# Handing phase products to operand tiles inside SBUF, and loading the first W blocks earlier, in an FFT convolution followed by token mixing

## The chip, the cores and the metric

The kernel runs on one core of one Trainium2 chip. The metric is the time of one execution on the device in microseconds (us). The profiled execution is one of the timed ones; its span is about 1.7 us shorter than its time.

In the lines of the profile PE is TensorE, DVE VectorE, ACT ScalarE, POOL GpSimd, and SPq the queue of SyncE, which issues DMAs; L833 is line 833 of the kernel, x4 a count, and m, b, zz, y_ap are tiles by their names in the program (b an operand tile, zz the products of a step). HBM is the memory outside the core, SBUF the core's own, PSUM the place where TensorE's sums arise. The *issue* of a DMA is the time that an engine takes to start it; it *lands* when its data has arrived. A wait is given to what ended it last.

## The reference

x is 8 × 5696 × 128 (batch, tokens S, channels), h is 5696 × 128, the two token-mixing matrices are 5696 × 5696 each.

```python
# stage 1: causal convolution along the tokens, by FFT of length 2*S
y  = irfft(rfft(x, 2*S) * rfft(h, 2*S)[None])[:, :S, :]
# stage 2
theta  = y @ w_theta
zr, zi = y * cos(theta), y * sin(theta)
u = y + einsum('ts,bsd->btd', w_tok_r, zr) + einsum('ts,bsd->btd', w_tok_i, zi)
out = u + relu(u @ w_ch)
```

## The kernel before

It has three parts that follow one another, with overlaps.

1. **FFT stages** (to about 462 us). The last inverse stage writes y, channel-major, to HBM (`yt_hbm`) and to SBUF.
2. **Phase steps** (in part beside the last inverse stage, then alone to about 550 us). One step handles 128 tokens of one half of the batch (4 of 8). The 22 token tiles of the first pass make 44 steps. A step transposes y, forms theta in PSUM, lets ScalarE take the sines and VectorE the products, writes y to HBM (`y2_hbm`), and hands zr and zi on, in two blocks of 64 tokens.
3. **Token mixing**, in two passes over the source tokens. The right-hand operand of a pass is 11 tiles b0 to b10, each of four blocks of 64 tokens, and of sums of its parts (the kernel multiplies by a scheme of seven products in place of eight; the very first visit, `tt == 0`, uses plain products while the sums are still being made). W comes in blocks, converted to bf16 by DMAs that GpSimd issues, into six slots, and is transposed by VectorE.

The hand-over from part 2 to part 3 goes through HBM: a step writes its products, and the tile is fetched whole after its last write.

```python
# in a phase step
def copy():
    nc.vector.tensor_copy(y_ap, tpz)
    nc.sync.dma_start(y2_hbm[ti]...[:, 512 * hh:512 * hh + 512], y_ap...)
...
nc.scalar.activation(mag, r, AF.Abs)
nc.scalar.activation(red, r, AF.Sin, bias=zero_b[:m], scale=-TWO_PI)
nc.scalar.activation(mag, mag, AF.Sin, bias=half_pi[:m], scale=-TWO_PI)
...
zi_eng.tensor_mul(zi, red, yflat)
nc.vector.tensor_mul(zr, mag, yflat)
for e in range((m + 63) // 64):                       # two blocks of 64 tokens
    ...
    nc.sync.dma_start(z_hbm[:, p_, j, i, :, cols].rearrange("z t n -> t z n"), zz[rows])
```

```python
# operand tiles; the eight early ones (NE) are fetched between the steps of the second half
def load_b(p, j, pool):
    t_ = pool.tile([P, 7 * 1024], BF16, tag=f"b{j}", name=f"b{j}")
    for z in range(2):
        eng = nc.scalar if p or j >= NE else nc.sync
        eng.dma_start(t_[:, z * 2048:(z + 1) * 2048],
                      z_hbm[z, p, j].rearrange("i (s r) n -> (i s) (r n)", r=2))   # rows of 4 KB
...
for n, ti in enumerate(tile_order):
    phase_step(ti, 1)
    if n % 4 == 3:
        while len(bts_of[0]) < min(n // 2, NE):
            load_b(0, len(bts_of[0]), bpe)
```

```python
# the first W blocks wait for an operand tile, so as not to crowd the phase steps
after = bts_of[0][2][M2][:, 0, :2] if k == 0 else None
...
if after is not None:
    nc.gpsimd.tensor_copy(wb[:, 0, :2], after)
for i in range(4):
    nc.gpsimd.dma_start(wb[32 * i:32 * i + 32, :ng, :nj * 64], bass.AP(tensor=a.tensor, ...))
```

## Time and profile before

| | before |
|---|---|
| median of the first 3 runs | 2174.2 us (2172.3 to 2176.88) |
| span of the profiled run | 2175.5 us |
| end of the last inverse stage (issue of the last write of yt) | 462.6 us |
| first product of the mixing | 549.4 us |
| TensorE busy, 600 to 800 us | 198.95 of 200 us |

The span is read as a chain of stretches. In the two passes TensorE is nearly full, so this change can pay only in the two places that it touches and where TensorE stands: between the last inverse stage and the first product, and around 1340 us, where the second pass fetches its 11 tiles. The prediction below shows the first place in full. For the second, these are TensorE's waits of the kernel before from 600 us to the end (engine, line, what it waited for, then us in total, times, longest):

```profile
PE m L833 <- DMA b<-z_hbm: 4.0, 2, 2.0
...
PE m L831 <- DMA b<-z_hbm: 0.4, 1, 0.4
```

And this is its DMA view from 1325 to 1370 us: the queue that carries the reload (packets, MB, share of the time of 16 engines), then the loads (KB each, median us from issue to landing).

```profile
q10 hardware_dynamic: 2568, 9.33, 53.3%
...
b<-z_hbm ACTq DMA_DIRECT2D x12, 512.0 KB, 11.1
```

TensorE loses 4.4 us to this reload, though it moves some 11.5 MB (22 loads of 512 KB).

### The profile page before, as it was taken

The page shows a single profiled execution, that of the slowest core. Times are in us where ns is not written, and L with a number is a line of the kernel's source. Part 1 is how long each engine was busy: PE and PEld are TensorE (multiplying, and loading weights), DVE is VectorE, ACT ScalarE, POOL GpSimd, SP SyncE. Part 2 cuts the span into 40 slices and gives each one's busy share as a digit, 9 for nine tenths or more (in the row PEclk, how much of TensorE's full clock was granted, in tenths as well). Part 3 has the DMA queues.
Part 4 walks back from the last instruction along what each step waited for, and adds up shares of the span by engine and source line. Part 5 has one row for each costly group of instructions (what it writes and reads, how often), then busy time and mean ns, then how long its engine had stood idle before and what let it go on. Part 6 is the DMA issues. An engine that isn't in the chain of part 4 may idle for free.

```text
span 2175.5 us, 41105 instructions
## 1 busy us (share of the span) xinstructions
PE 1998.2 (92%) x15545; PEld 1125.1 (52%) x15723; DVE 1619.4 (74%) x2920; ACT 670.6 (31%) x984; POOL 857.1 (39%) x1572
## 2 busy tenths in 40 slices
PE   4788898763899999999999999899999999999998
PEld 4787888652344444444444444344444444444444
DVE  7767767767778888888877667667777777776867
ACT  5877877574132333333210000001111111111111
POOL 5301010002344645445466544354545453535350
PEclk8788889987899999999999999999999999999999
DMA  7356463579988989899999869687878787879794
GB/s 146 89 125 163 128 162 118 172 185 275 236 156 175 182 169 168 167 179 176 176 169 162 138 115 291 106 133 137 148 132 152 132 151 130 152 131 153 126 158 91
DMA packets 409382, 340.38 MB, mean 156 GB/s; under 512 B 83303, under 2 KB 363751, under 8 KB 408071
## 3 DMA queue, kind: packets, MB, share of 16 engines
q0 software_dynamic: 221312, 143.00, 48.7%
q1 hardware_dynamic: 183552, 179.93, 28.5%
q10 hardware_dynamic: 4320, 14.81, 1.8%
q8 instruction: 123, 2.02, 0.4%
q14 instruction: 75, 0.61, 0.1%
HBM read 381.83 MB, written 97.93 MB: 221 GB/s over the span
## 4 chain that ended last, share of the span: by engine, by line
PE 65%; DMA 5%; DVE 4%; issue 2%; ACT 2%; POOL 1%; SPq 1%; DVEq 0%; ACTq 0%; POOLq 0%
PE m L910 59%; DMA b<-z_hbm 3%; PE m L878 2%; DMA z_hbm<-zz 2%; DVE c L917 1%; PE v L680 1%; PE utp L673 1%; PE m L914 1%; DVE wt L591 1%; PE m L833 1%; POOL wb L582 1%; PE m L831 1%; ACT mag L404 0%; ACT red L405 0%; PE theta_ps L382 0%
## 5 line engine op out<-in xcount | busy, mean ns | idle before, releaser
L582 POOL DMA_DIRECT2D wb<-in_moe_w_tok_i_dram x720 | 387.9, 547 | 679.3 <-DVE wt L591 602.6
L591 DVE STREAM_TRANSPOSE wt<-wb 128x384 f32<-128x384 f32 (+2 forms) x720 | 360.2, 524 | 117.1 <-PE m L910 71.2
L582 POOL DMA_DIRECT2D wb<-in_moe_w_tok_r_dram x720 | 386.6, 548 | 146.2 <-DVE wt L591 107.0
L910 PE MATMUL m<-b,wt 128*128 128x512 bf16 x1803 | 425.7, 381 | 7.1 <-DVE wt L591 2.4
L910 PEld LDWEIGHTS <-wt 128*128 128x128 bf16 x1848 | 181.3, 98 | 225.0 <-issue 5.7
L917 DVE TENSOR_TENSOR c<-c,m 128x512 f32<-128x512 f32 x420 | 271.0, 671 | 0.4 <-PE m L910 0.4
L675 ACT ACTIVATE uts<-utp 128x512 bf16<-128x512 bf16 (+1 forms) x90 | 53.2, 592 | 607.3 <-PE utp L673 607.3
L320 PE MATMUL ps<-r_u,u_t 128*128 128x128 f16 x1024 | 133.0, 228 | 14.9 <-DVE u_t L304 11.7
L321 PE MATMUL ps<-r_v,v_t 128*128 128x128 f16 x1024 | 131.7, 227 | 0.0
L670 ACT ACTIVATE ub<-c 128x512 bf16<-128x512 f32 (+1 forms) x90 | 56.3, 628 | 224.9 <-DVE c L846 139.7
L127 POOL DMA_DIRECT2D x<-in_x_dram x64 | 34.2, 541 | 201.3 <-PE ps L190 189.3
L320 PEld LDWEIGHTS <-u_t 128*128 128x128 f16 x1024 | 106.0, 103 | 13.6 <-DVE u_t L304 13.5
L321 PEld LDWEIGHTS <-v_t 128*128 128x128 f16 x1024 | 104.9, 103 | 5.2 <-issue 3.7
L304 DVE TENSOR_TENSOR u_t<-xs,hs 128x1024 f16<-128x1024 f16 x96 | 69.6, 725 | 41.9 <-ACT xs L302 31.5
L302 ACT ACTIVATE xs<-ps 128x1024 f16<-128x1024 f32 x96 | 95.3, 1017 | 17.6 <-DVE v_t L304 8.7
L878 PE MATMUL m<-b,wt 128*128 128x512 bf16 x344 | 79.3, 387 | 15.3 <-ACT red L405 14.5
L190 PE MATMUL ps<-f_t,x 89*128 89x180 f16 x512 | 84.5, 310 | 8.0 <-ACT xs L302 5.9
L208 PEld LDWEIGHTS <-w_t 64*128 64x128 f16 x3240 | 65.5, 106 | 38.1 <-issue 24.7
L580 POOL COPY wb<-b 128x2 bf16<-128x2 bf16 x4 | 0.5, 179 | 213.2 <-DMA z_hbm<-zz 213.2
L190 PEld LDWEIGHTS <-x 89*128 89x128 f16 x512 | 73.8, 237 | 10.1 <-issue 9.4
L384 ACT ACTIVATE red<-theta_ps,magic 128x512 f32<-128x512 f32 (+1 forms) x46 | 31.6, 687 | 140.8 <-PE theta_ps L382 107.4
L623 ACT ACTIVATE yb<-tpz 128x512 bf16<-128x512 bf16 (+1 forms) x46 | 27.4, 597 | 153.6 <-PE tpz L621 137.4
(2713 smaller groups left out, 3824.5 us busy)
## 6 DMA issues: line engine op xcount, KB each, us to landing
wb<-in_moe_w_tok_r_dram POOLq DMA_DIRECT2D x352, 96.0 KB, 4.5
wb<-in_moe_w_tok_i_dram POOLq DMA_DIRECT2D x352, 96.0 KB, 5.0
wb<-in_moe_w_tok_r_dram POOLq DMA_DIRECT2D x352, 80.0 KB, 4.2
wb<-in_moe_w_tok_i_dram POOLq DMA_DIRECT2D x352, 80.0 KB, 3.7
hs<-hf_hbm SPq DMA_DIRECT2D x192, 128.0 KB, 3.2
cp_hbm<-c SPq DMA_DIRECT2D x88, 256.0 KB, 2.3
c<-cp_hbm SPq DMA_DIRECT2D x88, 256.0 KB, 4.0
out_dram<-c SPq DMA_DIRECT2D x88, 256.0 KB, 4.2
```

Source lines behind the costliest of these rows:

```text
L190: nc.tensor.matmul(ps[:, i // 2, (i % 2) * 2 * K1:(i % 2 + 1) * 2 * K1], lhs(q + i), f1_t[:NB], start=True, stop=True)
L208: nc.tensor.matmul(ps[:, e, j * HD:(j + 1) * HD], w_t2[rows, c0 + j, N2 * (1 - ri):N2 * (3 - ri)], a_st["a"][rows, ri * K1 + c0 + j, :], s ...
L302: nc.scalar.activation(xs[:, :, :, :ck], ps, AF.Copy)
L304: nc.vector.tensor_tensor(uv[r][:, :, :, c0:c0 + ck], xs[:, :, :, :ck], hv[:, r:r + 1, :, :ck].to_broadcast([P, 2, HD, ck]), op=mult)
L320: nc.tensor.matmul(o, u_t[:, at:at + P], r_u, start=True, stop=False)
L321: nc.tensor.matmul(o, v_t[:, at:at + P], r_v, start=False, stop=True)
L582: nc.gpsimd.dma_start(wb[32 * i:32 * i + 32, :ng, :nj * 64], bass.AP(tensor=a.tensor, offset=a.offset + row0 * S + p * H + i * QR + j0 * 6 ...
L591: nc.vector.transpose(wt.rearrange("p j t r -> p (j t r)").bitcast(F32).rearrange("p (j g t) -> p g j t", j=TJ, g=4)[:, :ng, :nj], wb[:, : ...
L670: nc.scalar.activation(ub[:m].rearrange("p b d -> p (b d)"), c[:m], AF.Copy)
L878: nc.tensor.matmul(ms[n // 2 * 2 + h], a[n][:, j, :, r], bts[jj][n % 2 * 2 + h][:, r, :], start=(n % 2 == 0 and jj == 0 and r == 0), stop= ...
L910: nc.tensor.matmul(ms[q], a[q][:, j, :, r], bts[jj][q][:, r, :], start=(jj == 0 and r == 0), stop=(jj == NJ - 1 and r == 1 and q not in left))
L917: nc.vector.tensor_tensor(c, z, ms[q], op=op)
```

## The change

The intent is to take the HBM round trip out of the hand-over. For the second half of the batch, a step copies its products inside SBUF straight into the eight early tiles; the first half, which is written long before, is fetched in halves beforehand. So that such a half is contiguous, HBM holds the two halves of the batch apart, which makes the rows of every tile load 2 KB in place of 4 KB. The first six W blocks and tile b0 move into the room of the forward FFT's dead table, so that W can be loaded behind the last inverse stage.

```diff
-    z_hbm_h = nc.dram_tensor("z_hbm", (2, 2, 11, 4, 64, BD), BF16, kind="Internal")
+    z_hbm_h = nc.dram_tensor("z_hbm", (2, 2, 11, 2, 4, 64, BD // 2), BF16, kind="Internal")
...
-    w_t2 = fc.tile([P, K1, 3 * N2], F16)
+    w_t2 = keep.tile([P, K1, 3 * N2], F16, tag="keep", name="w_t2")
...
-            if tags is None:
-                nc.sync.dma_start(z_hbm[:, p_, j, i, :, cols].rearrange("z t n -> t z n"),
-                                  zz[rows])
+            if tags is None and j in home:
+                for r in range(2):
+                    nc.sync.dma_start(
+                        home[j][32 * i:32 * i + 32, :4096].rearrange("p (z q r n) -> p z q r n", z=2, q=2, r=2)[:, :, q_, r],
+                        zz[e * 64 + r:e * 64 + 64:2])
+            elif tags is None:
+                nc.sync.dma_start(z_hbm[:, p_, j, q_, i].rearrange("z t n -> t z n"), zz[rows])
...
+    def pump():
+        while ring["n"] < len(queue) and (ring["n"] < 6 or queue[ring["n"] - 6][0] in ring["read"]):
+            queue[ring["n"]][1]()
+    def open_ring():
+        ring["all"] = keep.tile([P, K1 * 3 * N2], BF16, tag="keep", name="ring")
+        pump()
...
+    def load_b_half(j):
+        t_ = home_of[j] = tile_b(0, j, bpe)
+        for z in range(2):
+            nc.sync.dma_start(t_[:, z * 2048:z * 2048 + 1024],
+                              z_hbm[z, 0, j, 0].rearrange("i (s r) n -> (i s) (r n)", r=2))
...
+    for j in range(NE - 1):
+        load_b_half(j)
     for step in steps0:
         step()
+    load_b_half(NE - 1)
     sides["phases"]["sby"] = pool("s2y4", 4, pha, reuse_waits="tile")
-    for n, ti in enumerate(tile_order):
+    for ti in tile_order:
         phase_step(ti, 1)
-        if n % 4 == 3:
-            while len(bts_of[0]) < min(n // 2, NE):
-                load_b(0, len(bts_of[0]), bpe)
... (the rest renames buffers, moves small buffers of the background work into the same room,
     and moves the queue of W loads into pump)
```

More of the change, by code (lines that the diff above doesn't have):

```diff
@@ L106 @@
     fx = pool("fft_x", 1, xin)
+    NE, WB, BT = 8, 6 * 4 * CJ * 64, 7 * 1024
+    keep = pool("keep", 1, ctx, side="right")
     fc = pool("fft_c", 1, conv, side="right")
@@ L169 @@
     cosine(f1_t[:NB, :K1], t, k)
-    w_t2 = fc.tile([P, K1, 3 * N2], F16)
+    w_t2 = keep.tile([P, K1, 3 * N2], F16, tag="keep", name="w_t2")
+    assert WB + BT + 3 * P * 2 <= K1 * 3 * N2
     def w_table(k0):
@@ L371, in phases_b @@
     def phases_b(ti, y_ap, b0, nb, yT, sb, th_pool, th_tag, zi_eng, turns=None, tags=("red", "mag"), m=P,
-                 theta_ps=None, copy=None):
+                 theta_ps=None, copy=None, home={}):
         n = nb * D
@@ L416, in phases_b @@
         cols = slice(b0 * D, b0 * D + n)
+        q_ = b0 // 4
         for e in range((m + 63) // 64):
@@ L428, in phases_b @@
             else:
                 for r, z in enumerate((zr, zi)):
-                    nc.sync.dma_start(z_hbm[r, p_, j, i, :, cols], z[rows])
+                    nc.sync.dma_start(z_hbm[r, p_, j, q_, i], z[rows])
+    CHUNKS = [(j0, min(CJ, NJ - j0)) for j0 in range(0, NJ, CJ)]
+    pairs = (list(range(21)) + [None, 21], [None] + list(range(22)))
+    chunks = [(p, tt, c) for p in range(2) for tt in pairs[p] for c in range(len(CHUNKS))]
+    ring = {"n": 0, "read": set(), "wl": 0}
+    loaded = {}
@@ new lines, in loads_of, with one @@
+    def loads_of(k):
+        p, tt, c = chunks[k]
+        loaded[k] = {}
+        def one(n, a, row0, ng):
+            loaded[k][n] = load_w(a, row0, p, *CHUNKS[c], ng=ng)
+        if tt is None:
+            return [lambda n=n, a=a: one(n, a, 2 * H, 2) for n, a in enumerate((moe_w_tok_r, moe_w_tok_i))]
+        src = [(a, h * H + tt * P, 4) for h in range(2) for a in (moe_w_tok_r, moe_w_tok_i)]
+        return [lambda n=n: one(n, *src[n]) for n in ((0, 1, 2, 3) if tt == 0 else (0, 3, 1, 2))]
@@ new lines, with small @@
+    queue = [(k, f) for k in range(len(chunks)) for f in loads_of(k)]
+    first_of = {}
+    for m, (k, _) in enumerate(queue):
+        first_of.setdefault(k, m)
+    def pump():
[4 more added lines that the diff above has]
+        pump()
+    def small(at, n):
+        return ring["all"][:, WB + BT + at:WB + BT + at + n]
@@ new lines, in wl_room, with yt_room, load_w @@
+    def wl_room():
+        ring["wl"] += 1
+        return small((4 + ring["wl"] % 2) * P, P)
+    def yt_room():
+        return small(0, 4 * P).rearrange("p (b n) -> p b n", b=4)
+    def load_w(a, row0, p, j0, nj, ng=4):
+        n = ring["n"] % 6
+        ring["n"] += 1
+        wb = ring["all"][:, n * WB // 6:(n + 1) * WB // 6].rearrange("p (g j) -> p g j", g=4)
+        for i in range(4):
+            nc.gpsimd.dma_start(
+                wb[32 * i:32 * i + 32, :ng, :nj * 64],
+                bass.AP(tensor=a.tensor,
+                        offset=a.offset + row0 * S + p * H + i * QR + j0 * 64,
+                        ap=[[S, 32], [32 * S, ng], [1, nj * 64]]))
+        return wb
@@ L473, in load_ya1 @@
                                   yt[64 * e:64 * e + 64].rearrange("p m n -> p (m n)")[:, :H])
+    home_of = {}
     def phase_step(ti, hh):
@@ L490, in phase_step @@
         phases_b(ti, y_ap, 4 * hh, 4, yT, st["sb1"], None, None, nc.vector, st["turns"], theta_ps=ps[:, 0, :],
-                 tags=None, copy=copy)
+                 tags=None, copy=copy, home=home_of if hh else {})
     tile_order = []
@@ L516, with tile_b @@
             load_ya1()
+            open_ring()
     conv.close()
-    CHUNKS = [(j0, min(CJ, NJ - j0)) for j0 in range(0, NJ, CJ)]
     M2, M6, M7, M5, M1, M3, M4 = range(7)
     ORDER = (M3, M4, M5, M2, M1, M7, M6)
-    wp = ctx.enter_context(tc.tile_pool(name="wpool", bufs=6, side="right"))
-    NE = 8
     bpe = ctx.enter_context(tc.tile_pool(name="bpool_e", bufs=1, side="right", reuse_waits="tile"))
     bts_of = {0: [], 1: []}
+    def tile_b(p, j, pool):
+        t_ = ring["all"][:, WB:WB + BT] if j == 0 else pool.tile([P, BT], BF16, tag=f"b{j}", name=f"b{j}")
+        bt = [t_[:, k * 1024:(k + 1) * 1024].rearrange("p (r n) -> p r n", r=2) for k in range(7)]
+        bts_of[p].append(bt)
+        return t_
     def load_b(p, j, pool):
-        t_ = pool.tile([P, 7 * 1024], BF16, tag=f"b{j}", name=f"b{j}")
+        t_ = tile_b(p, j, pool)
         for z in range(2):
-            eng = nc.scalar if p or j >= NE else nc.sync
-            eng.dma_start(t_[:, z * 2048:(z + 1) * 2048],
-                          z_hbm[z, p, j].rearrange("i (s r) n -> (i s) (r n)", r=2))
-        bt = [t_[:, k * 2048:(k + 1) * 2048].rearrange("p (r q n) -> p r q n", r=2, q=2)[:, :, q, :]
-              for k in range(2) for q in range(2)]
-        bt += [t_[:, q * 1024:(q + 1) * 1024].rearrange("p (r n) -> p r n", r=2) for q in range(4, 7)]
-        bts_of[p].append(bt)
+            nc.scalar.dma_start(
+                t_[:, z * 2048:(z + 1) * 2048].rearrange("p (q n) -> p q n", q=2),
+                z_hbm[z, p, j].rearrange("q i (s r) n -> (i s) q (r n)", r=2))
+    def load_b_half(j):
[3 more added lines that the diff above has]
+                              z_hbm[z, 0, j, 0].rearrange("i (s r) n -> (i s) (r n)", r=2))
     def sums_apart(bt):
@@ L574, in half @@
             return z[ti].rearrange("p b d -> p (b d)")[:, h * 512:h * 512 + 512]
-        def load_w(a, row0, p, j0, nj, ng=4, after=None):
-            wb = wp.tile([P, 4, CJ * 64], BF16, tag="wb")
-            if after is not None:
-                nc.gpsimd.tensor_copy(wb[:, 0, :2], after)
-            for i in range(4):
-                nc.gpsimd.dma_start(
-                    wb[32 * i:32 * i + 32, :ng, :nj * 64],
-                    bass.AP(tensor=a.tensor,
-                            offset=a.offset + row0 * S + p * H + i * QR + j0 * 64,
-                            ap=[[S, 32], [32 * S, ng], [1, nj * 64]]))
-            return wb
         def w_t(wb, j0, nj, ng=4, pool=None):
@@ L621, in first @@
                     nc.tensor.transpose(tpz[:m, b, :], st["yT"][:, b, :m], ident_bf)
-                st["yb"] = yb = cp.tile([P, 4, D], BF16, tag="yT", name="yb")
+                st["yb"] = yb = yt_room()
                 nc.scalar.activation(yb[:m], tpz[:m], AF.Copy)
@@ L658, in first @@
                                         ident_bf[:m, :m])
-                wls = cp.tile([P, 4, P], BF16, tag="yT", name="wls")
+                wls = yt_room()
                 nc.scalar.activation(wls[:, :n, :m], tpw[:, :n, :m], AF.Copy)
@@ L665, in u_stage, with first @@
             st = {}
-            def first(tags=("misc", "misc", "yT")):
+            def first(tags=("misc", "misc", None)):
                 st["tags"] = tags
@@ L673, in first @@
                     nc.tensor.transpose(utp[:, b, :m], ub[:m, b, :], ident_bf[:m, :m])
-                st["uts"] = uts = cp.tile([P, 4, P], BF16, tag=tags[2], name="uts")
+                st["uts"] = uts = cp.tile([P, 4, P], BF16, tag=tags[2], name="uts") if tags[2] else yt_room()
                 nc.scalar.activation(uts[:, :, :m], utp[:, :, :m], AF.Copy)
@@ L723, in start_pass @@
                 zl_of[p] = zl
-        pairs = (list(range(21)) + [None, 21], [None] + list(range(22)))
-        chunks = [(p, tt, c) for p in range(2) for tt in pairs[p] for c in range(len(CHUNKS))]
         stretches = []
@@ L732 @@
                 stretches.append((k, p, tt, j0, s0, min(TJ, nj - s0)))
-        loaded = {}
-        def loads(k):
-            if k >= len(chunks):
-                return
-            p, tt, c = chunks[k]
-            j0, nj = CHUNKS[c]
-            if tt is None:
-                loaded[k] = [load_w(a, 2 * H, p, j0, nj, ng=2) for a in (moe_w_tok_r, moe_w_tok_i)]
-            else:
-                top, bot = tt * P, H + tt * P
-                after = bts_of[0][2][M2][:, 0, :2] if k == 0 else None
-                src = ((moe_w_tok_r, top), (moe_w_tok_i, top), (moe_w_tok_r, bot), (moe_w_tok_i, bot))
-                got = {n: load_w(*src[n], p, j0, nj, after=after) for n in ((0, 1, 2, 3) if tt == 0 else (0, 3, 1, 2))}
-                loaded[k] = [got[n] for n in range(4)]
         def prepare(i, at_once=True):
@@ L752, in prepare, with read @@
             k, p, tt, j0, s0, nj = stretches[i]
-            if s0 == 0:
-                loads(k + 1)
+            pump()
+            def read():
+                if s0 + nj == CHUNKS[chunks[k][2]][1]:
+                    ring["read"].add(k)
+                    pump()
             if tt is None:
-                a1, a2 = (w_t(wb, s0, nj, ng=2) for wb in loaded[k])
+                a1, a2 = (w_t(loaded[k][n], s0, nj, ng=2) for n in range(2))
+                read()
                 return a1, a2, None if p else w_sum(a1, a2, add, nj, m=64)
-            w11, w12, w21, w22 = loaded[k]
+            w11, w12, w21, w22 = (loaded[k][n] for n in range(4))
             if tt == 0:
                 a = [w_t(w11, s0, nj), w_t(w12, s0, nj), w_t(w21, s0, nj, pool=sp), w_t(w22, s0, nj, pool=sp)]
+                read()
                 return a if at_once else (a, lambda n: None)
@@ L784, in prepare @@
                     step(n)
+                read()
                 return a
@@ L788 @@
         nxt, second, st = None, None, {}
-        loads(0)
         ordered = ExitStack()
@@ L839 @@
                     if zl is not None:
-                        wl = wlp.tile([P, P], BF16, tag="wl0", name="wl0")
+                        wl = wl_room()
                         nc.sync.dma_start(wl[:, :64], wl_hbm[:, NT - 1, :64])
@@ L853 @@
                 if zl is not None:
-                    wl = [wlp.tile([P, P], BF16, tag=f"wl{n}", name=f"wl{n}") for n in range(2)]
+                    wl = [wl_room(), wlp.tile([P, P], BF16, tag="wl1", name="wl1")]
                     for n in range(2):
```

## The prediction

> **What bounds the kernel now.** I read four views in this order: the busy time by stretches (to find where TensorE is not full), the waits of TensorE, the timeline of TensorE and VectorE in the stretch found, and the waits and timeline of the queue that issues DMAs (SPq). The first:
>
> ```profile
> core 0: us, PE busy (x) PEld busy (x) DVE busy (x) ACT busy (x) POOL busy (x), PEclk, DMA share, GB/s
> 462.00:505.00 43.00, 24.12 (x222) 17.14 (x224) 27.71 (x51) 27.46 (x49) 0.00 (x0) 0.80 0.85 224
> 505.00:560.00 55.00, 21.93 (x134) 12.88 (x136) 33.79 (x62) 18.08 (x31) 24.06 (x48) 0.66 1.12 283
> 560.00:600.00 40.00, 37.58 (x179) 17.32 (x182) 34.66 (x62) 8.07 (x13) 9.88 (x19) 0.96 0.88 212
> 600.00:800.00 200.00, 198.95 (x1013) 94.91 (x1031) 165.85 (x322) 66.64 (x107) 99.63 (x186) 1.00 0.93 171
> ```
>
> From 600 us on TensorE is busy 99.5% of the time: no change of transfers can win there, but whatever starts the multiplication earlier moves the end by as much. Between the last inverse stage (about 462) and 560 TensorE works 46 of 98 us, while the DMA engines are at a share of 0.85 and then 1.12. The waits of TensorE between 330 and 600 us say for what:
>
> ```profile
> PE ps L482 <- ACT red L405: 38.9, 22, 10.2
> PE m L878 <- ACT red L405: 14.5, 1, 14.5
> ```
>
> The phase steps (44 of them: 22 token tiles, two halves of the batch) hold PSUM tiles, and the multiplication gets its banks only when the last step has left them. In TensorE's timeline it starts at 549.4 and then runs without a gap up to the end of the first visit:
>
> ```profile
> 549.38 0.59 PE L878 MATMUL m<-b,wt 128*128 128x512 bf16 x1 [14.51 <-ACT red L405]
> 564.91 0.39 PE L621 MATMUL tpz<-ident_bf,yT 128*128 128x128 bf16 x4
> 565.13 5.34 PE L878 MATMUL m<-b,wt 128*128 128x512 bf16 x24
> ```
>
> So **the last phase step sets the start**, not the arrival of W or of the later operand tiles. Why the steps are slow: ScalarE is named, but it only comes last. VectorE, which works in order, stands still in between for operand tiles that come back from HBM, and SPq stands still before it may ask for them:
>
> ```profile
> DVE b L543 <- DMA b<-z_hbm: 11.3, 6, 4.6
> DVE y_ap L486 <- DMA y_hbm<-y_ap: 7.0, 3, 5.1
> SPq L534 <- DMA z_hbm<-zz: 9.8, 5, 3.6
> SPq L426 <- DMA b<-z_hbm: 5.1, 5, 1.8
> SPq L487 <- DMA b<-z_hbm: 4.6, 4, 1.7
> ```
>
> Undisturbed, a step goes at the pace of the issues, back to back on SPq:
>
> ```profile
> 484.32 0.59 SPq L487 DMA_DIRECT2D y_hbm<-y_ap  x1
> 485.01 1.24 SPq L426 DMA_DIRECT2D z_hbm<-zz  x2
> 486.30 0.59 SPq L487 DMA_DIRECT2D y_hbm<-y_ap  x1
> 486.99 1.23 SPq L426 DMA_DIRECT2D z_hbm<-zz  x2
> ```
>
> That is three issues in 1.97 us, 0.66 us each with the small gaps. ScalarE alone repeats a step every 1.66 us there.
>
> **What the Trainium skill says.** "Perfetto Trace Analysis", section What "DMA-bound" means, counts the issuing sequencer as a resource of its own: its track solid with DMA slices is descriptor generation, not data movement. The lines above agree (1.83 of 1.97 us). "DMA: Bandwidth & Descriptors", section Two DMAs through the same engine are not ordered, says that a DMA reading what another wrote must wait for its completion before it is issued; the 9.8 us of SPq at L534 are that wait. The same page, Why small descriptors are slow (HBM only), exempts SBUF-to-SBUF from the small-descriptor penalty; here the only such copies (yt into the second half's y, 64 rows) took 0.50 and 0.60 us to issue, and no row shows 1 KB pieces. "Perfetto Trace Analysis", DMA Optimizations, advises growing transfers from 2 to 4 KB; the change does the reverse for the tiles still loaded from HBM. The trace hints the same way: in the reload at 1325 to 1370 us, 9.33 MB in 2568 packets held 53.3% of 16 engines for 45 us, 149 ns per 3.6 KB, whereas packets near 1.6 KB in the stretch 386 to 402 us took about 90 ns, so some 37% more per byte, though under another load.
>
> **The change part by part.**
> (a) Early operand tiles. For the second half of the batch, 32 of the 44 blocks of 64 tokens go to their tile inside SBUF. One HBM write (0.62 us to issue) becomes two copies of 32 rows. The eight early tiles are no longer fetched whole after their last write (16 loads of 512 KB); their first half is fetched earlier (16 loads of 256 KB, two of them before the last inverse stage ends). This removes the write, wait, read chain: the 9.8 us of SPq, the 11.3 us of VectorE, and 4 MB of reads in the crowded stretch. The built order confirms that the three sums of a tile now stand one or more steps behind its last copy, with the one sum that needs the first half done early.
> (b) SPq. I count from the end of the issue of the last yt write, 464.6 us in both. Before: 56 z writes, 27 y writes, 16 loads = 99 issues, and the last ends at 555.1: 90.5 us, of which 99 x 0.63 = 62 us are issuing and the rest waits. After: 24 z writes, 64 copies, 27 y writes, 14 loads = 129 issues. With 0.65 us for z and y, 0.60 for a copy (as the SBUF copies above) and 0.47 for a load: 15.6 + 38.4 + 17.6 + 6.6 = 78 us, so 543 us if nothing waits. The multiplication starts some 6 us before the last issue, as before (549.4 against 555.1, four buffers of slack): 537. I add 1 to 3 us for the start, where twelve half loads (3 MB, near 350 GB/s some 9 us) stand ahead and VectorE waits for them. Start of the multiplication: **about 539 us, 10 us earlier**.
> (c) W blocks. The first six blocks are loaded once the forward table is dead, about 412 us, instead of from 511. That takes 24 DMAs (2.3 MB) out of the stretch with a DMA share of 1.12 and puts them where it is 0.6 to 0.67. It helps (a) keep its pace; by itself it is worth nothing, because the transposes of W were done (539 to 543) before 549. Its later loads reuse the same six slots in the same turn, so the steady state stays.
> (d) The second pass loads all 11 tiles as 2 KB rows. There TensorE waits 2.0, 0.5 and 2.0 us for them and the DMA engines are saturated at about 350 GB/s. Dearer packets may add 0 to 4 us: I take +1.5.
> VectorE's operand tiles become contiguous; its sums already take 0.68 us for 1024 elements in both layouts, so nothing. Sum: -10 + 1.5 = -8.5, I round to **-10**, since less traffic also shortens the waits for y. 2174 - 10 = **2164 us**.
>
> **Rivals.**
> 1. The issue queue does not bind as I think: a copy of 32 rows issues in about 0.45 us like the loads, or the copies hide. Then the bound is VectorE: 27 steps of 1.56 us, 24 sums of 0.61 and 9 transposes of 0.5 are 61 us, so the multiplication starts near 528. For it: loads issue at 0.41 to 0.52. Against: every SBUF-source row shows 0.5 or more. Time about 2152.
> 2. The chain is only renamed: each copy lands after 2 to 3 us, the queue allows eight in flight, and VectorE waits in order for copies and half loads. Multiplication starts near 548, and with (d) the time is 2174 to 2177. For it: 30 more issues, and stalls of 5 us even at 467 to 473 without any operand load. Against: DMA traffic falls, and the waits in question are for 512 KB reads.
> 3. One large tile as the ring of W, early tile and small scratch ties transfers that were independent, and the steady state suffers. It could cost 20 us or more. The built program speaks against it: each transpose waits for its own four DMA lanes, and the blocks take the slots in the same order.
> 4. The change wins everything up to ScalarE's pace: 27 x 1.66 = 45 us, a start at 510, 39 us saved. Even that is under 2% (43.5 us), so faster by over 2% is almost out.
>
> **Range and chances.** Rival 1 gives the lower end, 2147 with a little more; rival 2 the upper, 2177. In between I lean to the queue bound. Faster by over 2% needs more than rival 4 offers: 0.02. Slower by over 2% needs rival 3 in force: 0.02. Within 2%: 0.96.
>
> **What would show it.** Right: the first multiplication (m<-ring) starts at 533 to 545; SPq is nearly solid from 480 to 540 with five issues per step, about 3 us; the wait of SPq for z_hbm writes before loads of early tiles is gone, VectorE's wait for b loads falls below 5 us and lies before 485; W loads appear from about 412; TensorE stays above 99% from 600 shifted. Wrong: copies that issue in 0.4 us or less (rival 1), VectorE waiting long for b<-zz (rival 2), TensorE below 99% in the steady stretch (rival 3), or a reload of the second pass that costs more than 5 us extra (then (d) was undersized). If the start moves by 10 us and the end does not, the argument that the rest only shifts is wrong.

## The result, and the profile after

The changed kernel takes **2187.69 us** (median of 4 runs, 2184.33 to 2189.88), beside 2173.25 us for the kernel before (4 runs, 2172.23 to 2176.88). The ratio is **1.0062**, with a 95% interval of 1.0043 to 1.0081. Ratios here are the mean time of one kernel's fast runs over that of the other's of the same rounds, so not quite the ratio of the medians. The output is correct. The change is slower by 0.6%: inside the class "within 2%", but outside the predicted range of 2147 to 2177 us, and in the opposite direction from the predicted 10 us of gain.

The two profiled spans are 2175.5 and 2182.6 us, only 7.1 us apart, because the profiled run of after was its fastest. I therefore profiled both kernels once more later (e9 and e10 below: 2175.2 and 2184.3 us). All four are cut at the same marks, in us:

| stretch | before | before again | after | after again |
|---|---|---|---|---|
| A: from the first loads of y for the phase steps to the issue of the last yt write | 87.8 | 89.2 | 89.1 | 90.9 |
| B: from there to the first product | 86.8 | 86.1 | 89.8 | 91.2 |
| V: first visit | 41.5 | 40.6 | 41.6 | 40.8 |
| P0: rest of the first pass | 747.3 | 746.1 | 743.4 | 744.2 |
| R: last group of products of the first pass to first full product of the second | 29.5 | 29.5 | 34.6 | 35.6 |
| P1: rest | 807.8 | 807.8 | 807.5 | 807.9 |

(What is missing to the span is the part before A, 373.6 to 376.6 us here, which the change does not touch and which varies from run to run.) Two stretches are clearly longer, B by 3 to 5 us and R by 5 to 6; P0 is shorter by 2 to 4 us. B was to be 10 us shorter.

The busy time by stretches of the kernel after has the columns that the prediction explains (window, its length, then busy us and counts of PE, PEld, DVE, ACT, POOL, then clock, DMA share, GB/s):

```profile
462.00:505.00 43.00, 19.72 (x185) 14.11 (x186) 24.86 (x44) 20.73 (x38) 0.00 (x0) 0.72 0.81 227
505.00:560.00 55.00, 28.74 (x175) 18.94 (x180) 38.38 (x70) 28.44 (x48) 8.59 (x16) 0.57 0.64 144
...
600.00:800.00 200.00, 198.00 (x1007) 94.52 (x1027) 165.56 (x321) 65.14 (x105) 100.78 (x188) 1.00 0.95 174
```

The transfers did go away: from 505 to 560 us the DMA share fell from 1.12 to 0.64 and the traffic from 283 to 144 GB/s. The steady stretch from 600 us stays at 99%. But from 462 to 505 us TensorE does less than before (19.7 against 24.1 us), and the first product starts at 555.41 us, 6.0 us later than before. TensorE's waits from 330 to 600 us of the kernel after:

```profile
PE ps L547 <- ACT red L408: 38.4, 26, 9.1
PE m L923 <- ACT red L408: 11.7, 1, 11.7
```

The picture is the same as before: the last phase step sets the start. What sets the pace of the steps now is seen in the timeline of SPq, the queue that issues DMAs (start, us, line, what it moves, how many issues). First the half loads that stand in front of the second half's steps, then one full step:

```profile
474.41 7.33 SPq L608 DMA_DIRECT2D b<-z_hbm  x12
...
523.89 0.53 SPq L552 DMA_DIRECT2D y_hbm<-y_ap  x1
524.52 2.55 SPq L431 DMA_DIRECT2D b<-zz  x4
527.17 0.53 SPq L552 DMA_DIRECT2D y_hbm<-y_ap  x1
```

A step now has five issues and repeats after 3.28 us (523.89 to 527.17); before, it had three in 1.97 us. The queue is nearly solid, with gaps of 0.1 us. VectorE's waits in the window from 462 to 563 us of the kernel after show what this does to it:

```profile
DVE zz L417 <- DMA b<-zz: 8.0, 6, 2.1
DVE y_ap L551 <- DMA y_hbm<-y_ap: 6.9, 4, 5.0
...
DVE b L614 <- DMA b<-z_hbm: 5.2, 4, 3.4
DVE b L613 <- DMA b<-zz: 3.8, 2, 3.5
```

Before, VectorE waited 11.3 us for operand tiles. Now it waits 8.0 us for a product buffer that copies have not left yet, 3.8 us to add what a copy brings, and 5.2 us for half loads.

In the reload, TensorE's waits from 600 us on are now these:

```profile
PE m L878 <- DMA b<-z_hbm: 6.3, 3, 3.5
...
PE m L876 <- DMA b<-z_hbm: 1.4, 1, 1.4
```

That is 7.7 us in place of 4.4. The DMA view from 1325 to 1380 us:

```profile
q10 hardware_dynamic: 4921, 9.47, 49.3%
...
b<-z_hbm ACTq DMA_DIRECT2D x16, 512.0 KB, 12.2
```

A packet took 49.3% × 16 × 55 us / 4921 = 88 ns for 1.92 KB, 46 ns per KB. Before it was 53.3% × 16 × 45 us / 2568 = 149 ns for 3.63 KB, 41 ns per KB. Smaller rows cost 11% more engine time per byte, and a load of 512 KB lands after 12.2 in place of 11.1 us.

W is indeed loaded early (GpSimd's timeline, from 402.5 us; in the kernel before, from about 511 us):

```profile
402.52 2.20 POOL L488 DMA_DIRECT2D ring<-in_moe_w_tok_r_dram  x4 [105.50 <-PE ps L211]
```

### The profile page after: what moved, and what is told of

The parts are those of the page before. It is cut to its first block, busy times and chain, and to the rows that moved or that the text cites. A ratio compares the mean times of both kernels' runs of the same rounds, so it can differ in the third digit from the quotient of the medians.

```text
span 2182.6 us, 41147 instructions
## 1 busy us (share of the span) xinstructions
PE 2001.5 (92%) x15545; PEld 1126.8 (52%) x15723; DVE 1621.6 (74%) x2920; ACT 670.6 (31%) x984; POOL 856.0 (39%) x1568
## 4 chain that ended last, share of the span: by engine, by line
PE 65%; DVE 5%; DMA 4%; issue 2%; ACT 1%; SPq 1%; POOL 0%; DVEq 0%; ACTq 0%
PE m L955 59%; DMA b<-z_hbm 2%; PE m L923 2%; DVE c L962 2%; DVE wt L648 1%; PE v L737 1%; PE utp L730 1%; PE m L959 1%; DMA y_hbm<-y_ap 1%; DMA b<-zz 1%; PE m L878 0%; PE m L876 0%; PE theta_ps L385 0%; ACT red L408 0%; PE tpz L678 0%
## 5 line engine op out<-in xcount | busy, mean ns | idle before, releaser
L488 POOL DMA_DIRECT2D ring<-in_moe_w_tok_i_dram x720 | 387.8, 546 | 675.6 <-DVE wt L648 598.3
L488 POOL DMA_DIRECT2D ring<-in_moe_w_tok_r_dram x720 | 386.2, 545 | 371.4 <-DVE wt L648 219.4
L648 DVE STREAM_TRANSPOSE wt<-ring 128x384 f32<-128x384 f32 (+2 forms) x720 | 359.9, 524 | 114.4 <-PE m L955 64.6
L955 PE MATMUL m<-b,wt 128*128 128x512 bf16 x1638 | 394.2, 380 | 3.3 <-DVE wt L648 0.9
L732 ACT ACTIVATE ring<-utp 128x512 bf16<-128x512 bf16 (+1 forms) x86 | 50.9, 592 | 607.5 <-PE utp L730 607.5
L680 ACT ACTIVATE ring<-tpz 128x512 bf16<-128x512 bf16 (+1 forms) x46 | 27.4, 597 | 155.9 <-PE tpz L678 135.5
L923 PE MATMUL m<-b,wt 128*128 128x512 bf16 x314 | 72.6, 386 | 0.4 <-issue 0.2
L739 DVE SCALAR_TENSOR_TENSOR c<-v,c 128x512 f32<-128x512 f32 (+1 forms) x90 | 61.4, 684 | 11.7 <-PE v L737 11.6
```

Of the source, the lines that this page charges most:

```text
L648: nc.vector.transpose(wt.rearrange("p j t r -> p (j t r)").bitcast(F32).rearrange("p (j g t) -> p g j t", j=TJ, g=4)[:, :ng, :nj], wb[:, : ...
L739: nc.vector.scalar_tensor_tensor(c[:m], v[:m], 0.0, c[:m], op0=ALU.max, op1=ALU.add)
L923: nc.tensor.matmul(ms[n // 2 * 2 + h], a[n][:, j, :, r], bts[jj][n % 2 * 2 + h][:, r, :], start=(n % 2 == 0 and jj == 0 and r == 0), stop= ...
L955: nc.tensor.matmul(ms[q], a[q][:, j, :, r], bts[jj][q][:, r, :], start=(jj == 0 and r == 0), stop=(jj == NJ - 1 and r == 1 and q not in left))
```

## The experiments

**Theory.** In stretch B the number of DMA issues on SPq sets the pace, and there are more of them than before (129 against 99 after the last yt write); in R the 2 KB rows cost what the table shows. **Rivals** for B: the block of twelve half loads holds up the first steps of the second half; the early W loads disturb; or it is the landing of the copies, not their issue, that VectorE waits for. Each experiment changes one of these. The first four ran on one chip, the next four on another, the last three on a third.

### e1: the second pass keeps its 4 KB rows

```diff
+    z1_hbm = nc.dram_tensor("z1_hbm", (2, 11, 4, 64, BD), BF16, kind="Internal").ap()
-                    nc.sync.dma_start(z_hbm[r, p_, j, q_, i], z[rows])
+                    nc.sync.dma_start(z1_hbm[r, j, i, :, cols] if p_ else z_hbm[r, p_, j, q_, i], z[rows])
 # load_b and the views of a tile for p == 1: as in the kernel before, from z1_hbm
```

> The changed kernel, but the second pass keeps the old layout in HBM, so its 11 operand tiles are again loaded as 4 KB rows. If the narrower 2 KB rows are what slowed the reload (from the last product of the first pass to the first full product of the second: 28.7 us before, 33.8 us changed), that stretch falls back to about 29 us and the time by about 5 us, to some 2182. If the reload is longer only because the ring shifted the W loads into it, both stay where they are: 34 us and 2187.

Measured: 2182.06 us, ratio to before 1.0007 (0.9984 to 1.0031). Stretch R is 27.0 us, under both the kernel before (29.5) and the kernel after (34.6 and 35.6). P0 is 747.4 us here, some 3 to 4 more than in the kernel after, so P0 and R together are 774.4 us against 778.0 and 779.8: 3.7 to 5.4 us less. TensorE's waits in the reload:

```profile
PE m L886 <- DMA b<-z_hbm: 3.5, 1, 3.5
```

B does not move (90.0 us). It follows that the 2 KB rows make R longer, and that they explain nothing of B. All profiles agree: R is 32.3 to 37.5 us in the eight with 2 KB rows, and 27.0 to 29.8 in the five with 4 KB rows (before, e9, e1, e6, e7). Why e1 loses some us again in P0 is open; of these, 1.6 us are one wait for a sum on VectorE.

### e2: the copies are issued by GpSimd

```diff
-                    nc.sync.dma_start(
+                    nc.gpsimd.dma_start(
                         home[j][32 * i:32 * i + 32, :4096]...
```

> The changed kernel, but the 64 copies into the early operand tiles are issued from the GpSimd queue, which is idle from 429 to 546 us; SyncE keeps 65 of its 129 issues. If the issue of DMAs on one queue sets the pace of the phase steps (3.28 us a step, of which five issues of 0.64 us), a step falls to about 2.1 us, where VectorE and ScalarE bind, and the first product starts near 537 instead of 555: time down by 15 to 20 us, to 2168 to 2173. If the wait for copies to land (VectorE waited 11.8 us for them) is the cause, the start stays at 550 to 557 and the time within 4 us of 2187.

Measured: 2170.22 us, ratio 0.9953 (0.9927 to 0.998), faster than before. B falls to **73.9 us**, by 16 to 17 us. The copies, their bytes and the products are the same as in the kernel after; only the queue that issues them differs. GpSimd's timeline shows their issue at 0.52 us each:

```profile
506.76 4.19 POOL L431 DMA_DIRECT2D b<-zz  x8 [1.63 <-DVE zz L418]
...
542.24 1.05 POOL L431 DMA_DIRECT2D b<-zz  x2 [3.30 <-DVE zz L418]
543.28 2.20 POOL L488 DMA_DIRECT2D ring<-in_moe_w_tok_r_dram  x4
```

The queue now waits for VectorE, and no longer VectorE for it: the row "DVE zz L417 <- DMA b<-zz" (8.0 us in the kernel after) is gone from VectorE's waits altogether. The copies do not land sooner: from the start of the issue to the landing they take 2.62 us (median) here, against 2.13 in the kernel after. In the busy time by stretches VectorE is at 46.7 of 55 us from 505 to 560 us, against 38.4:

```profile
505.00:560.00 55.00, 34.46 (x253) 20.22 (x253) 46.70 (x86) 29.68 (x51) 38.21 (x73) 0.88 0.84 201
```

The last line of GpSimd's timeline shows a cost: the next W loads stand behind the copies on the same queue and go out only at 543.3 us. V grew to 46.2 us, some 5 us more; TensorE waits there 3.3 us for a background phase step ("PE theta_ps L385 <- ACT ring L680"). That the two belong together was not tested.

### e3: the half loads spread over the steps

```diff
-    for j in range(NE - 1):
+    for j in range(2):
         load_b_half(j)
...
-    load_b_half(NE - 1)
-    for ti in tile_order:
+    for n, ti in enumerate(tile_order):
+        if n % 2 == 0 and len(home_of) < NE:
+            load_b_half(len(home_of))
         phase_step(ti, 1)
```

> The changed kernel, but the half loads of the early tiles are put one tile per two phase steps instead of twelve loads in a row at 474 us. If that block of loads, with VectorE's sums waiting behind it, costs its stretch (474 to 488 us) some 6 to 9 us, the first product starts near 548 and the time falls by about 6. If the queue bound only swallows it (129 issues remain, each 0.64), the start moves by 2 us or less.

Measured: 2185.19 us, ratio 1.0032 (1.0004 to 1.0061); B is 89.6 us, within what the kernel after shows (89.8 and 91.2). VectorE's waits for copies fell from 8.0 to 4.2 us, but the start did not come earlier. The number of issues is the same; putting them elsewhere gains nothing. The block of half loads is not the cause, although the queue does spend 7.3 us on it.

### e4: the first W blocks held back

```diff
     def open_ring():
         ring["all"] = keep.tile([P, K1 * 3 * N2], BF16, tag="keep", name="ring")
-        pump()
...
+        if ring["n"] <= 6:
+            nc.gpsimd.tensor_copy(wb[:, 0, :2], bts_of[0][0][1][:, 0, :2])
...
         phase_step(ti, 1)
+    pump()
```

> The changed kernel, but the first six W blocks are held back until the first early tile is complete (about 510 us), as the kernel before did. If the early W loads help the phase stretch by lowering its DMA share, the first product now starts 3 us or more later. If they only crowd the last inverse stage (it ended 1.3 us later after them) it starts 1 to 2 us earlier. If they matter for nothing, start and time stay within 1 us and 3 us of the changed kernel.

Measured: 2187.83 us, ratio 1.0037 (1.0011 to 1.0064). A is 89.4 us and B 92.0. W starts at 508.2 us here. Held back, it neither restores the start nor delays it by much: B is 1 to 2 us longer than in the kernel after, and A lies between its two profiles (89.1 and 90.9).

### e5: twice as many copies, of half the size

```diff
-                    nc.sync.dma_start(home[j]...[:, :, q_, r], zz[e * 64 + r:e * 64 + 64:2])
+                    for z_ in range(2):
+                        nc.sync.dma_start(home[j]...[:, z_, q_, r], zz[e * 64 + r:e * 64 + 64:2, z_])
```

> The changed kernel, but each copy into an early tile is split in two, the same bytes in the same 1 KB pieces: 193 issues on SyncE after the last yt write in place of 129. If the number of issues sets the pace (0.64 us each), the stretch from that write to the first product grows from 89.7 by 64 x 0.64 = 41 us, to about 131, and the time by the same, to about 2228. If the bytes or the landing of the copies set it, the smaller copies change it by less than 5 us.

Measured: 2222.24 us, ratio **1.0201** (1.0182 to 1.0221). B is **127.7 us**, 37.9 more than in the profile of the kernel after, for 64 more issues and not a byte more: 0.59 us per issue. In the queue's timeline a copy of half the size costs the same as the whole one did (4.98 / 8 = 0.62 us, against 2.55 / 4 = 0.64):

```profile
539.66 4.98 SPq L432 DMA_DIRECT2D b<-zz  x8
544.74 0.53 SPq L553 DMA_DIRECT2D y_hbm<-y_ap  x1
```

And VectorE's wait for product buffers grew with it:

```profile
DVE zz L417 <- DMA b<-zz: 26.6, 8, 4.3
```

The count of issues, not the bytes, sets the pace.

### e8: only the y writes go to GpSimd

```diff
-            nc.sync.dma_start(y2_hbm[ti]...
+            (nc.gpsimd if hh else nc.sync).dma_start(y2_hbm[ti]...
```

> The changed kernel, but the 22 writes of y in the second half are issued from the GpSimd queue; the copies stay on SyncE, which keeps 107 of 129 issues. If the queue's issues set the pace, the step falls from 3.28 to about 2.6 us and the stretch from the last yt write to the first product from 89.7 by about 14 us, to 76; the time falls to about 2174. If it was the copies' landing that VectorE waited for (and which moving the copies to another queue happened to shorten), the stretch stays near 90.

Measured: 2176.08 us, ratio 0.999 (0.9961 to 1.0018). B is 80.7 us: 22 issues fewer on SPq make 9 to 10.5 us, in the direction expected but short of the 14 us. The copies stay where they are, on SPq, and VectorE still waits less for them:

```profile
DVE zz L417 <- DMA b<-zz: 2.8, 2, 1.7
```

Had the landing of the copies been the limit, moving the writes of y would not be expected to help. The doses together (SPq issues after the last yt write, then B):

| kernel | issues on SPq | B, us |
|---|---|---|
| e2, e6, e7 | 65 | 73.9, 73.4, 74.6 |
| e8 | 107 | 80.7 |
| after, twice; e3 | 129 | 89.8, 91.2; 89.6 |
| e5 | 193 | 127.7 |

From 107 issues up the slope is 0.4 to 0.6 us per issue. From 107 down to 65 it is only 0.16: there something else takes over.

### e6 and e7: a version that beats both

e6 puts e1 and e2 together; e7 adds e3.

> Both repairs together: the copies on the GpSimd queue and the 4 KB rows for the second pass. If the two losses are separate, the gains add: about 10 us faster than before for the copies (as measured with them alone) and 3 to 5 us more for the rows, so some 2165 and 0.992 to 0.994 of the kernel before. If the reload only follows what came ahead of it, nothing is gained over the copies alone (0.995).

> The version with both repairs, plus the half loads spread over the phase steps. With 129 issues on SyncE spreading moved nothing. If that was because the queue swallowed it, now that the queue has slack the block of twelve loads shows: the stretch to the first product falls from 74 by 4 to 7 us and the time by the same, below the version with both repairs. If the block is harmless anyway, both take the same time within 2 us.

Measured: e6 takes **2166.4 us**, ratio to before 0.994 (0.9917 to 0.9964), and e7 2168.91 us, ratio 0.9943 (0.9914 to 0.9972). e6 has B at 73.4 and R at 27.3 us, e7 74.6 and 29.8. Both are faster than the kernel before by 0.6%; spreading the half loads adds nothing here either (the first visit of e7 takes 48.3 us, that of e6 43.9). TensorE's waits from 330 to 600 us in e6 show what the bound is by then:

```profile
PE ps L548 <- ACT red L409: 30.8, 21, 8.2
PE m L931 <- DVE wt L656: 8.2, 1, 8.2
```

The first product waits for VectorE, which has W still to transpose between the products of the last steps, and works without a pause from 523.4 us to the first product at 538.3. W has long been there, so the wait is for VectorE's turn; loading it early cannot help.

### e9 to e11: before, after and e4 once more

No edit; one profile each, in single runs whose state is unknown.

> The kernel before, unchanged, profiled once more, to see how far single profiles scatter. The stretch from the four loads of the first half of y (near 375 us) to the last yt write took 87.8 us in the first profile. If the early W blocks are what lengthens it (89 to 93 us in eight profiles with early W), it stays at 87 to 89 here. If it is scatter, it may come out anywhere up to 93.

> The changed kernel, unchanged, profiled once more. With early W the stretch to the last yt write should be near the mean of the eight such profiles, 91.6 us; the stretch from there to the first product 89 to 91 us, and the reload 34 to 35 us, as in its first profile.

> The version with W held back, unchanged, profiled once more. It took 89.4 us up to the last yt write and 92.0 from there to the first product. If holding W back gives to the first stretch what it takes from the second, both come out within 1.5 us of that again: the first below 90, the second above 91.

Measured: 2176.99, 2186.08 and 2187.41 us, beside 2180.34 us for a run of the kernel before on the same chip. The stretches of e9 and e10 stand in the table above and repeat. e11 has A at 89.4, B at 92.2 and R at 35.9 us. Taking all profiles: A is 88.9 us on average in the four where W is not loaded early (before, e9, e4, e11) and 91.5 in the nine where it is. So early W costs some 2.6 us of the last inverse stage and brings back 1 to 2.4 us in B: about nothing in sum.

## Why the prediction was wrong

**The reading of the bound held.** The prediction said that the last phase step sets the start, that nothing can be won from 600 us on, and that issues on SPq would set the pace of the steps. After the change all three are so, and e2, e5 and e8 show the last. Two parts of what was to show it right are in the trace: five issues per step in about 3 us (3.28), and W loads early (from 402.5 us, where 412 was said).

**Step (b) failed: the sum of the issues was taken for the length of the stretch.** It said: 129 issues are 78 us, so the queue ends at 543 if nothing waits, plus 1 to 3 us. The queue went from 467.65 to 562.4 us, 94.7 us. Of the missing 17 us, about 7 are the pace: in the middle 77 issues went at 0.66 us each, gaps included, and 129 × 0.66 = 85 us; the copies were put at 0.60 without their gaps. About 10 us are waits, mainly at both ends: the first 32 issues took 28.3 us and the last 20 took 15.7. The kernel before had shown 90.5 us for 99 issues, which are 65 us at the same pace (62 in the prediction), so some 25 us of waits; the prediction assumed that the change would remove all but 1 to 3 of these. It removed about 15 and added 30 issues, which is some 20 us. So the queue took 4 us longer, and B 3 in this pair, in place of −10. The mechanism was right; the terms that were mis-sized are the waiting that stays and, less so, the pace. What the queue still waits for is a mix (its largest entry is 2.3 us, for VectorE's copies of y), and no run takes it apart. The sum of −8.5 us had also been rounded to −10 because the waits for y would shorten; these stayed (7.0 us before, 6.9 after).

**Step (a) was half right.** SPq's wait of 9.8 us for z_hbm writes is gone, as said. VectorE's 11.3 us for tiles did not go: 17.0 us (8.0 + 3.8 + 5.2) of waits for copies and half loads took its place. This is what rival 2 looks like, and rival 2 also came nearest in size (start near 548, 2174 to 2177 us; measured 555.4 and 2187.7). But its reason, the landing of each copy, is refuted: in e2 the same copies land in the same tiles, in the median 0.5 us later after their issue, and yet the waits of 8.0 us vanish once another queue issues them. A wait for a copy was mostly a wait for its turn to be issued.

**Step (d) was undersized.** It took +1.5 us with 0 to 4 possible; R grew by 5.1 and 6.1 us, and with 4 KB rows (e1) it is 27.0 us. The prediction's own list names "more than 5 us" as the sign. TensorE's longer wait for tiles is 3.3 us of it in the profiled pair (7.7 against 4.4). Part of the rest is slower products: after these waits they stand 0.43 us apart in place of 0.22, 12 times against 6, some 1.3 us, and the granted clock over R is 0.80 against 0.88. The rate per byte was, on the contrary, overestimated (37%, or 34% when its figures are not rounded first, against the measured 11%). So it was not the rate that was set too low; that the reload had no slack left, since it already ended behind the work that hides it, is my reading of the waits of 4.4 us before.

**Step (c)** called the early W loads worth nothing by themselves, and they are, in sum. It missed that they lengthen A by about 2.6 us. **Rival 1** is refuted (copies issue in 0.64 us, not 0.45), **rival 3** too (99% from 600 us on, and P0 even 2 to 4 us shorter). That gain was not predicted. In it TensorE's waits for VectorE fell from 4.8 to 2.5 us (those for transposed W from 2.6 to 1.1). It appears in every variant with the new ring but e1 (747.4 us), and no run here separates its cause. **Rival 4** stayed far off: even with 65 issues on SPq, B is 73.4 us, and by then the first product waits for VectorE.

The sum of the profiled pair: +1.3 in A, +3.0 in B, +0.1 in V, −3.9 in P0, +5.1 in R, −0.3 in P1, and +1.8 before A that varies from run to run, together 7.1 us. The timed runs differ by 13.5 us in the mean. The later pair (9.1 us) lies between; the rest is within what single runs vary, and I do not assign it.

## What to carry to other kernels

Before replacing one transfer by several smaller ones, count the issues on the queue that has to start them: a transfer that avoids HBM still costs its issue (0.64 us here), and where the queue sets the pace, that decides. When a queue's issues are added up to forecast a stretch, allow for waiting that stays: here about 10 of 25 us did. To scale by the old ratio of stretch to sum (90.5 / 62) would have overshot: 114 us for the 78, against 94.7 measured. And a reload in which TensorE already waits a few us is a warning that dearer packets may show in the time, as the 2 KB rows did here.

## What the Trainium skill lacked or had wrong

- "DMA: Bandwidth & Descriptors", section Issuing engines are not separate DMA queues, says that issuing from several engines saves only the sequencer's time, "which is usually small relative to the DMA itself". Here it was not small: the same copies issued by GpSimd instead of SyncE cut stretch B from 89.8 to 73.9 us, though each landed later (2.62 against 2.13 us).
- The same page, section Why small descriptors are slow (HBM only), exempts SBUF-to-SBUF copies from the penalty on bytes, but has no word there on what such a copy costs to issue: 0.64 us on SyncE, and 0.62 for half the size (e5). Elsewhere the page has a cycle count for generations before trn3, but no time measured on this chip.
- The same page, section Issuing engine by pattern, calls DMAs from sync and scalar generally faster than those from gpsimd. For these copies that held from issue to landing (2.13 us on SyncE, 2.62 on GpSimd), but not for the issue, which took 0.52 us on GpSimd and 0.64 on SyncE.
- "Perfetto Trace Analysis", section DMA Optimizations, is right in advising larger transfers and in balancing issues across engines (e1 and e2), but gives no size for rows of 2 KB against 4 KB. In this reload it was 46 against 41 ns per KB, and 5 to 6 us of stretch R.
